# Root steps with a per-partition scalar in place of a second tensor, and a fill that begins on zeros

## The chip, the cores and the metric

One core of a Trainium2 chip runs the whole kernel as one program. The metric is the device time of one execution in microseconds (us), the median of the runs shown. A core has five engines that run beside each other, each through its own instructions in order: TensorE (PE, matrix products; loading of its weights is shown apart as PEld), VectorE (DVE), ScalarE (ACT), GpSimd (POOL) and SyncE (SP, which here issues nearly all transfers). They wait for one another by semaphores.

## The reference

Attention over 2048 tokens of width 1024 (32 heads of 32), gated by a mixture-of-depths feed-forward of eight routed tokens; both work on the layer-normalised input.

```python
xn = _layernorm(x, axis=-1)            # (x - m) / sqrt(v + 1e-5)
s = _A_ref(xn, A_wqkv, A_wo)           # softmax attention, then @ wo
g = _silu(_B_ref(xn, B_w_r, B_w_gate, B_w_up, B_w_down))   # top-8 tokens through a SwiGLU FFN
return x + s * g
```

## The kernel before, in words

The 2048 tokens are 16 tiles of 128 (t = 0 to 15), four tiles to a block. The instructions of all engines are put in order by hand: what Python calls first stands first in its engine's queue.

**The head**, the first 81 us, normalises the tiles and turns them so that features lie on partitions, in two half-precision parts (a high part and a residue, the low part). For each tile `ln_stats` takes mean and variance on DVE (two instructions of 512 columns and one that merges them), `ln_root` makes 1/sqrt(var + eps), `ln_apply` normalises (tile 0 on DVE, the others on ACT). `ln_root` starts with a square root on ACT and returns a list of short DVE steps, run one after the other by `rest()`: a reciprocal y of the root, then vy = (var + eps) * y, w = -0.5 * vy * y, r = (w + 1.5) * y, which is one Newton step, and nmr = -mean * r. From tile 4 on (`wide`) a last step `by` scales r and nmr by 64 with one TENSOR_SCALAR of two columns (L181). All of them work on 128 partitions and one column, `by` on two.

Tiles 0 to 3 are turned by PE (`ln_turn`). Tiles 4 to 15 are turned by DMA: `ln_high` writes the high part on ACT (L217), `ln_turn_dma` lets POOL subtract it from the tile (L223, a two-input TENSOR_TENSOR of 128 x 1024) and then issues a transposing DMA on SP (L226).

One pass of the loop over t in `_fast` calls, in this order: `ln_apply(t+1)`, the square root of tile t+2, `ln_high(t+1)`, PE's products that are due, then `rest()` (the DVE steps of tile t+2), the low part of an early tile, `ln_turn_dma(t+1)`, `ln_stats(t+3)`, the moves (stores and loads on SP that had become due) and the evictions of finished products. So ACT has the square root of one tile in front of the high part of the tile before it; DVE has a tile's steps in front of the next tile's statistics; SP has the transpose in front of stores and loads.

PE meanwhile makes keys, queries and values of the first heads from the turned tiles (`chain`, `chain_v`), in the order of the tiles. Where it has nothing yet, filling products are put: `turn_over(count)` multiplies the identity with itself into a PSUM tile that nobody reads, 13 times before the first tile, then 9 and 6 times more. An fp32 product runs as two passes, so 13 of them are 26 instructions.

**The rest**, from 81 us on, loops over 8 groups of four heads, 4 blocks of queries and 16 tiles of keys: scores on PE, exponentials on ACT, a running sum on DVE, values on PE, with projections, the feed-forward and the output projection put in between.

The identity is built on DVE at the very start, by seven doubling additions, a transposition and a comparison. The pool tag `o32` has two buffers, first used by the attention's output at the end of the first block of queries.

Of the kernel before, what the change touches and what calls it, by code (L numbers as in the profile page):

```python
# [9 lines left out]
F32 = mybir.dt.float32  # L10
# [4 lines left out]
ALU = mybir.AluOpType  # L15
# [3 lines left out]
P = 128  # L19
# [6 lines left out]
EPS = 1e-5  # L26
# [29 lines left out]
@with_exitstack  # L56
def kernel(ctx, tc, x, wqkv, wo, w_r, w_gate, w_up, w_down, out,
                                      general=True, force_general=False):
    nc = tc.nc
    x = x.rearrange("b s d -> (b s) d")  # L60
    out = out.rearrange("b s d -> (b s) d")

    dram = ctx.enter_context(tc.tile_pool(name="dram", bufs=1, space=bass.MemoryType.DRAM))
    keep = ctx.enter_context(tc.tile_pool(name="keep", bufs=1))
    y_d = dram.tile([C, D], F32, name="y_d")
    slot_d = dram.tile([P, NT], I32, name="slot_d")
    ok_i = keep.tile([P, 1], I32, name="ok_i")

    with ExitStack() as st:
        _fast(st, tc, x, wqkv, wo, w_r, w_gate, w_up, w_down, out, dram, y_d, slot_d, ok_i,  # L70
              force_general)

    if general:
        ok = nc.values_load(ok_i[0:1, 0:1], min_val=0, max_val=P)
        with tc.If(ok < P):
            with ExitStack() as st:
                _general(st, tc, x, wqkv, wo, out, dram, y_d, slot_d)
# [28 lines left out]
def _fast(ctx, tc, x, wqkv, wo, w_r, w_gate, w_up, w_down, out, dram, y_d, slot_d, ok_i,  # L106
          force_general):
    nc = tc.nc
    const = ctx.enter_context(tc.tile_pool(name="const", bufs=1))
    sb = ctx.enter_context(tc.tile_pool(name="sb", bufs=1))  # L110
# [4 lines left out]

    ident = const.tile([P, P], F32, name="ident")
    num = sb.tile([P, 2, P], F32, name="num", tag="rb", bufs=1)
    nc.vector.memset(num[:, 0, 0:1], 0.0)  # L120
# [14 lines left out]
    rstd_r, nmr = rn[:, 0], rn[:, 1]  # L135
# [13 lines left out]
    def wide(t):  # L149

        return t >= T_DMA
# [20 lines left out]
    def ln_root(t):  # L172

        tmp = small.tile([P, 4], F32, name="rsq", tag="rsq", bufs=3)
        root, y, vy, w = (tmp[:, i:i + 1] for i in range(4))
        mean, var, r = mv_r[:, t, 0:1], mv_r[:, t, 1:2], rstd_r[:, t:t + 1]
        stt = nc.vector.scalar_tensor_tensor
        nc.scalar.activation(root, var, AF.Sqrt, bias=eps, scale=1.0)
        if wide(t):
            by[t] = small.tile([P, 2], F32, name="by", tag="by", bufs=2)  # L180
        more = [lambda: nc.vector.tensor_scalar(by[t], rn[:, :, t], XS, None, op0=ALU.mult)] if wide(t) else []  # L181
        return [lambda: nc.vector.reciprocal(y, root),
                lambda: stt(vy, var, EPS, y, op0=ALU.add, op1=ALU.mult),
                lambda: stt(w, vy, -0.5, y, op0=ALU.mult, op1=ALU.mult),
                lambda: stt(r, w, 1.5, y, op0=ALU.add, op1=ALU.mult),
                lambda: stt(nmr[:, t:t + 1], mean, -1.0, r, op0=ALU.mult, op1=ALU.mult)] + more

    def ln_apply(t, act):
        xn = LN[t]
# [624 lines left out]
    for g in range(NG):  # L814
        n = g + 1
# [143 lines left out]

    warm = psm.tile([P, 4, P], F32, name="warm", tag="m")  # L960

    def turn_over(count):
        for n in range(count):
            nc.tensor.matmul(warm[:, n % 4, :], ident, ident, start=True, stop=True)

    turn_over(13)

    load_x(0)
    load_x(1)
# [15 lines left out]

    ln_stats(0)
    steps += ln_root(0)
    for _ in range(4):
        step1()
    ln_apply(0, False)  # L990
    step1()
    w_high(1, 0)
    ln_stats(1)
    steps += ln_root(1)
    rest()
    ln_turn(0)
    turn_over(9)
    ln_apply(1, True)
    w_low(1, 0)
# [6 lines left out]
    todo += ks[2:3]  # L1006
    run(400)
    turn_over(6)
    ln_stats(2)
    steps += ln_root(2)  # L1010
    w_low(2, 0)
    rest()
# [281 lines left out]
```

## Time and profile before

| | us |
|---|---|
| median of 3 runs | 1621.5 |
| lowest and highest | 1621.48, 1623.89 |
| the profiled execution | 1622.08 |
| its span, first to last instruction | 1620.2 |
| mean granted clock of TensorE in it | 0.999 of full speed |

The span is shorter than the execution's time by what lies before its first and behind its last instruction. Times in the rows below are counted from the start of the span.

### The profile page before, as it was taken

Reading aid. Unit: us, or ns where it says so; the run is one execution under the profiler, and the core shown is the slowest. Engines: PE = TensorE matmul, PEld = TensorE weight load, DVE = VectorE, ACT = ScalarE, POOL = GpSimd, SP = SyncE. Lnnn points to the kernel's source line nnn. Section 1 sums busy time; section 2 is a strip of 40 time slices with the busy share of each in tenths; the row PEclk is TensorE's granted clock in tenths of the full one; section 3 lists DMA queues with packets and bytes.
Section 4 is the critical chain, followed back from the end, with each engine's and each line's share of the span. In section 5 each row is a group of like instructions: output and inputs, shape, how many; then the busy total and the mean of one; then the engine's idle time right before and its main releaser. Section 6 shows DMA issues by size and latency. Waiting matters only on the chain.

```text
span 1620.2 us, 59634 instructions
## 1 busy us (share of the span) xinstructions
PE 1604.8 (99%) x27193; PEld 816.8 (50%) x27193; DVE 1399.5 (86%) x1128; ACT 1177.2 (73%) x1312; POOL 148.2 (9%) x145
## 2 busy tenths in 40 slices
PE   8999999999999999999999999999999999999998
PEld 7744444444454444444455555555444444455555
DVE  8578999999999998898998988888898999987872
ACT  6677778777787777787877887677777878665530
POOL 3400000000000000000000000000000102030310
PEclk9999999999999999999999999999999999999999
DMA  9935555455644454556655577689788888656533
GB/s 292 203 105 139 140 150 149 135 138 140 176 126 90 116 144 124 138 152 162 170 137 138 137 219 204 173 227 236 209 226 218 236 216 222 212 143 187 180 127 120
DMA packets 250109, 273.68 MB, mean 169 GB/s; under 512 B 107994, under 2 KB 196362, under 8 KB 246010
## 3 DMA queue, kind: packets, MB, share of 16 engines
q1 hardware_dynamic: 239338, 242.10, 51.6%
q0 software_dynamic: 10512, 27.70, 10.8%
q8 instruction: 214, 3.51, 0.9%
q14 instruction: 45, 0.37, 0.1%
HBM read 195.98 MB, written 103.34 MB: 185 GB/s over the span
## 4 chain that ended last, share of the span: by engine, by line
PE 90%; DMA 4%; issue 3%; DVE 2%; SPq 1%; ACT 1%; POOL 0%; POOLq 0%; ACTq 0%; DVEq 0%
PE sc L276 25%; PE oa L421 25%; PE proj L276 17%; PE wop L276 10%; PE vp L276 8%; DMA a_d<-a_d 2%; PE ffn L638 1%; PE vp L323 1%; DMA a_d<-pt 1%; DMA xt<-xh 1%; PE py L669 1%; DMA wraw<-in_A_wqkv_dram 0%; DVE stt L168 0%; DMA wd<-in_B_w_down_dram 0%; PE proj L300 0%
## 5 line engine op out<-in xcount | busy, mean ns | idle before, releaser
L407 ACT ACTIVATE pt<-sc 128x1024 f32<-128x1024 f32 x1024 | 998.3, 1025 | 333.3 <-PE sc L276 249.8
L414 DVE TENSOR_TENSOR pt<-pt 128x2048 f32<-128x2048 f32 x480 | 1095.8, 2285 | 53.2 <-ACT pt L407 30.4
L276 PE MATMUL sc<-qs,ks 128*32 128x512 f16 x8192 | 617.2, 379 | 1.2 <-ACT pt L407 1.2
L421 PE MATMUL oa<-pt,v 128*32 128x512 f32 x4096 | 530.2, 592 | 0.0
L276 PE MATMUL proj<-xt,w 128*32 128x512 f16 x5664 | 417.4, 379 | 0.0
L276 PEld LDWEIGHTS <-ks 128*32 128x32 f16 x8192 | 226.5, 97 | 171.4 <-issue 19.8
L276 PEld LDWEIGHTS <-w 128*32 128x32 f16 x5664 | 155.9, 97 | 238.4 <-issue 139.2
L457 POOL DMA_DIRECT2D a_d<-a_d x90 | 73.0, 811 | 1242.6 <-DMA a_d<-pt 926.0
L276 PEld LDWEIGHTS <-xt 128*32 128x32 f16 x4608 | 125.3, 97 | 108.2 <-issue 79.5
L421 PEld LDWEIGHTS oa<-pt,v 128*32 128x32 f32 x4096 | 127.1, 110 | 100.6 <-ACT o L432 0.4
L276 PE MATMUL wop<-wo,ot 128*32 128x512 f16 (+1 forms) x3168 | 172.7, 373 | 0.0
L276 PE MATMUL vp<-w,xt 128*32 128x256 f16 x4608 | 172.1, 273 | 0.0
L276 PEld LDWEIGHTS <-ot 128*32 128x32 f16 x3168 | 94.2, 97 | 87.2 <-issue 22.4
L374 DVE SCALAR_TENSOR_TENSOR hl<-proj,hl 128x512 f16<-128x512 f32 x61 | 42.0, 689 | 57.6 <-ACT hl L373 57.5
L788 DVE SCALAR_TENSOR_TENSOR z<-wop,z 128x512 f32<-128x512 f32 (+1 forms) x33 | 21.9, 669 | 39.7 <-PE wop L276 39.7
L323 PE MATMUL vp<-w,xt 128*128 128x256 f16 x384 | 43.9, 273 | 2.7 <-DMA xt<-xh 2.6
L323 PEld LDWEIGHTS <-xt 128*128 128x128 f16 x384 | 37.1, 98 | 8.8 <-DMA xt<-xh 3.3
L373 ACT ACTIVATE hl<-proj 128x512 f16<-128x512 f32 x61 | 36.3, 595 | 4.8 <-PE proj L276 3.6
L638 PE MATMUL ffn<-wf,xst 128*32 128x224 f32 x512 | 35.7, 352 | 0.0
L638 PEld LDWEIGHTS ffn<-wf,xst 128*32 128x32 f32 x512 | 16.1, 110 | 38.8 <-issue 37.4
L260 DVE SCALAR_TENSOR_TENSOR w<-wraw,w 128x1024 f16<-128x1024 f32 x23 | 28.0, 1217 | 5.0 <-ACT w L255 5.0
L499 DVE SCALAR_TENSOR_TENSOR ohl<-o,ohl 128x512 f16<-128x512 f32 x28 | 19.3, 690 | 11.9 <-ACT ohl L497 11.9
(145 smaller groups left out, 589.8 us busy)
## 6 DMA issues: line engine op xcount, KB each, us to landing
a_d<-pt SPq DMA_DIRECT2D x30, 1024.0 KB
st<-hl SPq DMA_DIRECT2D x64, 256.0 KB
ks<-st SPq DMA_DIRECT2D x128, 128.0 KB
qs<-st SPq DMA_DIRECT2D x128, 128.0 KB
a_d<-a_d POOLq DMA_DIRECT2D x30, 512.0 KB, 6.6
wf<-in_B_w_gate_dram SPq DMA_DIRECT2D x32, 448.0 KB
wf<-in_B_w_up_dram SPq DMA_DIRECT2D x32, 448.0 KB
wd<-in_B_w_down_dram SPq DMA_DIRECT2D x32, 448.0 KB
```

The lines of the kernel that those rows point to most:

```text
L260: nc.vector.scalar_tensor_tensor(hl[:, 1], WR[c, g], WS, hl[:, 0], op0=ALU.mult, op1=ALU.subtract)
L276: nc.tensor.matmul(out[c], w[:, c], x, **flags)
L323: nc.tensor.matmul(box["ps"][:, tt], xt[:, xi, k, t % 4 * P:(t % 4 + 1) * P], w[:, :, wi, k, :], start=(n == 0), stop=(n == 23))
L373: nc.scalar.activation(hl[:, 0], ps, AF.Copy, scale=KQ)
L374: nc.vector.scalar_tensor_tensor(hl[:, 1], ps, KQ, hl[:, 0], op0=ALU.mult, op1=ALU.subtract)
L407: nc.scalar.activation(PT[u][:, 2 * hf:2 * hf + 2], ps, AF.Exp, bias=0.0, scale=ESC)
L414: nc.vector.tensor_add(ACC[g, qb], ACC[g, qb], PT[u])
L421: nc.tensor.matmul(OA[g, qb][32 * j:32 * j + 32, :], VT[g, kt // 2][:, kt % 2, 32 * j:32 * j + 32], PT[u][:, j, :], start=(kt == 0), stop= ...
L457: nc.gpsimd.dma_start(a_d[0:n], a_d[n:2 * n], accum_op=ALU.add, max_dma_last_dim=4096)
L499: nc.vector.scalar_tensor_tensor(hl[:, 1], o32, OS, hl[:, 0], op0=ALU.mult, op1=ALU.subtract, accum_out=lo_f[:, n:n + 1])
L638: nc.tensor.matmul(box[i][32 * j:32 * j + 32, :], RT["xst"][:, k, :], wt[:, j * FQ:(j + 1) * FQ], start=(k == 0), stop=(k == KT - 1))
L788: nc.vector.scalar_tensor_tensor(z, box[nh][:, c0:c0 + width], WOD, z, op0=ALU.mult, op1=ALU.mult)
```

## The change

Two edits. In `ln_root` the four steps between the reciprocal and `by` become `tensor_scalar` in place of `scalar_tensor_tensor`: the last operand, a column of 128 values, is read as a per-partition scalar and not as a second tensor. And the first filling products no longer multiply the identity but a tile of zeros, `blank`, which DVE writes as its first instruction in a buffer of the tag `o32`; there are 14 of them in place of 13. The two later fills stay on the identity.

```diff
+    blank = sb.tile([P, P], F32, name="blank", tag="o32", bufs=2)
+    nc.vector.memset(blank, 0.0)
     ident = const.tile([P, P], F32, name="ident")
...
-        stt = nc.vector.scalar_tensor_tensor
+        ts = nc.vector.tensor_scalar
...
         return [lambda: nc.vector.reciprocal(y, root),
-                lambda: stt(vy, var, EPS, y, op0=ALU.add, op1=ALU.mult),
-                lambda: stt(w, vy, -0.5, y, op0=ALU.mult, op1=ALU.mult),
-                lambda: stt(r, w, 1.5, y, op0=ALU.add, op1=ALU.mult),
-                lambda: stt(nmr[:, t:t + 1], mean, -1.0, r, op0=ALU.mult, op1=ALU.mult)] + more
+                lambda: ts(vy, var, EPS, y, op0=ALU.add, op1=ALU.mult),
+                lambda: ts(w, vy, -0.5, y, op0=ALU.mult, op1=ALU.mult),
+                lambda: ts(r, w, 1.5, y, op0=ALU.add, op1=ALU.mult),
+                lambda: ts(nmr[:, t:t + 1], mean, -1.0, r, op0=ALU.mult, op1=ALU.mult)] + more
...
-    def turn_over(count):
+    def turn_over(count, src=ident):
         for n in range(count):
-            nc.tensor.matmul(warm[:, n % 4, :], ident, ident, start=True, stop=True)
-
-    turn_over(13)
+            nc.tensor.matmul(warm[:, n % 4, :], src, src, start=True, stop=True)
+
+    turn_over(14, blank)
```

## Rows read from the trace of the kernel before

**Rows 1.** The page's busy times by engine, with shares of the span and numbers of instructions.

```profile
PE 1604.8 (99%) x27193; PEld 816.8 (50%) x27193; DVE 1399.5 (86%) x1128; ACT 1177.2 (73%) x1312; POOL 148.2 (9%) x145
```

**Rows 2.** The waits of PE over the whole span: who waited for whom, us in total, times, the longest.

```profile
PE vp L323 <- DMA xt<-xh: 2.6, 2, 1.4
```

**Rows 3.** The chain of waits over the first 100 us, in order of time: start, us, what. A DMA's time is from its issue to its landing.

```profile
38.68 6.22 DMA xt<-xh
...
75.76 5.36 DMA xt<-xh
...
81.17 2.79 PE vp L323 x24
```

**Rows 4.** The timeline of one turn of the head, of all engines but PE: start, us, engine, line, operation, out<-in, count, and in brackets the idle time before it and what ended it. The steps belong to tile 6, POOL's subtraction to tile 5.

```profile
32.12 0.29 ACT L178 ACTIVATE rsq<-mv_r,eps 128x1 f32<-128x1 f32 x1 [1.16 <-DVE mv_r L170]
32.33 1.04 ACT L217 ACTIVATE xh<-xin 128x1024 f16<-128x1024 f32 x1
32.45 0.16 DVE L182 RECIPROCAL rsq<-rsq 128x1 f32<-128x1 f32 x1 [0.36 <-ACT rsq L178]
...
33.42 0.17 DVE L181 TENSOR_SCALAR by<-rn 128x2 f32<-128x2 f32 x1
33.44 2.15 POOL L223 TENSOR_TENSOR xh<-xin,xh 128x1024 f16<-128x1024 f32 x1 [1.92 <-DVE rn L186]
...
35.06 0.29 ACT L178 ACTIVATE rsq<-mv_r,eps 128x1 f32<-128x1 f32 x1 [0.19 <-DVE mv_r L170]
```

**Rows 5.** Line L181 by itself: how often, duration in ns (least, median, most), first and last start in us.

```profile
L181 DVE TENSOR_SCALAR by<-rn x12: 169/169/2056, 25.2 to 63.8; 128x2 f32<-128x2 f32 x12
```

**Rows 6.** The timeline of the last two turns, columns as in rows 4.

```profile
58.69 2.12 POOL L223 TENSOR_TENSOR xh<-xin,xh 128x1024 f16<-128x1024 f32 x1 [0.80 <-ACT xh L217]
58.78 2.06 DVE L181 TENSOR_SCALAR by<-rn 128x2 f32<-128x2 f32 x1
...
62.50 0.29 ACT L178 ACTIVATE rsq<-mv_r,eps 128x1 f32<-128x1 f32 x1
...
63.80 0.17 DVE L181 TENSOR_SCALAR by<-rn 128x2 f32<-128x2 f32 x1
63.81 2.15 POOL L223 TENSOR_TENSOR xh<-xin,xh 128x1024 f16<-128x1024 f32 x1 [3.00 <-DVE rn L186]
...
66.47 2.13 POOL L223 TENSOR_TENSOR xh<-xin,xh 128x1024 f16<-128x1024 f32 x1 [0.51 <-ACT xh L217]
```

**Rows 7.** DVE's groups by line and shape over the whole span: count, then busy us, mean ns of one, and idle us before them. L516 is the routing's dot product, whose scalar is the tile's mean; L744 has an immediate. L677 multiplies by a per-partition gate; L644 and L1131 have immediates. L184 is a root step.

```profile
L744 DVE SCALAR_TENSOR_TENSOR z<-up,z 128x1024 f32<-128x1024 f32 x16 | 19.4, 1220 | 3.7 <-ACT up L743 3.7
...
L516 DVE SCALAR_TENSOR_TENSOR xr<-xr,mv_r,wr_bc 128x1024 f32<-128x1024 f32 x16 | 20.4, 1278 | 0.0
...
L184 DVE SCALAR_TENSOR_TENSOR rsq<-rsq 128x1 f32<-128x1 f32 x16 | 2.5, 159 | 0.6
...
L644 DVE TENSOR_SCALAR fe<-fe 128x224 f32<-128x224 f32 x4 | 1.1, 273 | 0.3 <-ACT fe L643 0.3
...
L677 DVE TENSOR_SCALAR y<-y,gate 128x256 f32<-128x256 f32 x1 | 0.4, 353 | 0.0
...
L1131 DVE TENSOR_SCALAR fl<-fl 128x1 f32<-128x1 f32 x1 | 0.1, 147 | 0.0
```

**Rows 8.** The timeline around POOL's two instructions on a weight tile (L265 with one tensor input, L266 with two), columns as in rows 4.

```profile
19.56 2.82 POOL L265 TENSOR_SCALAR wraw<-wraw 128x1024 f32<-128x1024 f32 x1 [19.10 <-ACT w L255]
...
21.57 0.16 DVE L183 SCALAR_TENSOR_TENSOR rsq<-mv_r,rsq 128x1 f32<-128x1 f32 x1
...
22.46 2.14 POOL L266 TENSOR_TENSOR w<-wraw,w 128x1024 f16<-128x1024 f32 x1
...
24.37 0.25 DVE L183 SCALAR_TENSOR_TENSOR rsq<-mv_r,rsq 128x1 f32<-128x1 f32 x1
```

**Rows 9.** The timeline of the first turn with a subtraction on POOL, columns as in rows 4; the square root is tile 5's.

```profile
28.06 0.29 ACT L178 ACTIVATE rsq<-mv_r,eps 128x1 f32<-128x1 f32 x1 [1.13 <-DVE mv_r L170]
...
29.36 0.17 DVE L181 TENSOR_SCALAR by<-rn 128x2 f32<-128x2 f32 x1
29.38 2.14 POOL L223 TENSOR_TENSOR xh<-xin,xh 128x1024 f16<-128x1024 f32 x1 [4.77 <-ACT xh L217]
```

**Rows 10.** SP's queue between the transposes of tiles 14 and 15: start and us of the issuing, columns as in rows 4.

```profile
72.91 2.15 SPq L389 DMA_DIRECT2D ks<-st  x4
75.11 0.54 SPq L332 DMA_DIRECT2D v_d<-vs  x1
```

**Rows 11.** A stretch behind tile 4's transpose: its length, then busy us (and instructions) of each engine, the granted clock, the busy share of the DMA engines, GB/s.

```profile
35.50:36.00 0.50, 0.50 (x4) 0.24 (x3) 0.40 (x4) 0.50 (x1) 0.09 (x1) 1.00 0.00 0
```

**Rows 12.** The timeline of the start, columns as in rows 4.

```profile
0.82 0.06 DVE L120 MEMSET num<- 128x1 f32 x1 [0.82 <-PEq L1283]
0.86 0.09 DVE L130 MEMSET ones<- 128x32 f32 x1
...
3.19 4.57 PE L964 MATMUL warm<-ident 128*128 128x128 f32 x26 [3.19 <-DVE ident L126]
...
3.78 0.69 DVE L168 BATCH_NORM_STATS2 stt<-xin 128x6 f32<-128x512 f32 x1 [0.64 <-DMA xin<-in_A_x_dram]
```

**Rows 13.** The filling passes by themselves, between 5 and 5.5 us and between 6.5 and 7 us: count, duration in ns (least, median, most), first and last start.

```profile
L964 PE MATMUL warm<-ident x5: 421/421/421, 4.6 to 5.5; 128*128 128x128 f32 x5
...
L964 PE MATMUL warm<-ident x7: 275/275/275, 6.3 to 6.9; 128*128 128x128 f32 x7
```

## The prediction

> **What bounds the kernel now.** I read the page's busy shares first. TensorE (PE) is busy for 1604.8 of 1620.2 us [rows 1], and in the waits of PE the only long ones are for the identity at the start [rows 12] and for two landings of transposed tiles [rows 2]. So what the change does to the time is what it does to the moment at which PE gets its last input of the head (the first 81 us); after that PE's order is fixed and nearly gapless, and a shift at 81 us goes through to the end. I then read the chain of waits over the head. Up to 33 us it runs through VectorE (DVE): the root steps of tile after tile, with the statistics between them; then through GpSimd's subtraction (POOL, L223), SP's queue and the transposes. PE waits last at 81.17 us, for the landing of tile 15, whose transpose SP issued at 75.76 us, 5.41 us earlier [rows 3].
>
> Next I read the timeline of one tile's turn, where the changed steps stand [rows 4]. At 32.12 ACT starts a square root; call that moment s. At s+0.20 ACT starts the high half of the tile before (L217), which ends at s+1.24, and POOL's subtraction starts 0.08 later, at s+1.32. Meanwhile DVE does the reciprocal (s+0.33), four short steps and "by" (L181) at s+1.30. So "by" starts 0.02 us ahead of POOL. It is so in ten turns of eleven, from 29.36 against 29.38 in the first to 63.80 against 63.81 in the last, never by more than 0.04 [rows 6, 9]. In the eleventh a DVE eviction had come between, and "by" started at 58.78, 0.09 us after POOL at 58.69. It took 2.06 us, until 60.84, when POOL's 2.12 were over [rows 6]; the median of L181 is 169 ns [rows 5]. On that view I stake the forecast: "by" that comes in front of POOL is free, "by" that comes behind it waits for the whole subtraction.
>
> **The change part by part: the steps.** Four steps of each of 16 roots become TENSOR_SCALAR with one immediate and one per-partition scalar. The trace has no such form with one column, so I bound it. TENSOR_SCALAR with immediates alone takes 147 ns at one column; the old form takes 159. What a per-partition scalar adds is seen at other sizes. SCALAR_TENSOR_TENSOR of 1024 columns takes 1278 ns with one and 1220 without: +58. TENSOR_SCALAR of 256 columns with one takes 353, and 224 columns without take 273: +80, or +42 if the 32 columns more cost 1.2 ns each, the other operation's rate (1220 over 1024) [rows 7]. So a step takes 147 ns at the least and 147+80 = 227 at the most. I take 209, as the closest pair (one operation, one size, with and without) says about 60: +50 ns a step, 0.20 us a root.
>
> **What 0.20 us a root costs by itself.** Tile 0's root is hidden behind a weight split on ACT. Roots 1 to 4 lie on the chain: 0.80 us, less 0.09 because tile 4's first step at 24.37 lasted 0.25 (it ended with POOL's L266) [rows 8] and would now start as that ends. So s of tile 5 moves from 28.06 [rows 9] to about 28.8.
>
> **What it costs through POOL.** From there on "by" would start at s+1.50 and POOL still at s+1.32, since POOL waits for ACT's L217, which waits for nothing of DVE's behind s. So "by" ends with POOL, at s+1.32+2.14+0.02 = s+3.49 instead of s+1.47: 2.02 us later, in each of the ten turns that escaped until now. Behind "by" on DVE stand the next tile's statistics, behind these the next square root; ACT waits for "by" with the tile's normalisation. From the end of "by" to the next square root it is 1.47 us [rows 4], so the period becomes 4.95, against 2.94 where DVE alone set it. Other turns were longer, as ACT's evictions stood in them; these now fit into ACT's new wait, so I count periods and not additions. From tile 5 to tile 6 it was 4.06 (a residue step stands behind "by") and becomes 6.08 [rows 4, 9]. Then come nine periods of 4.95, and tile 15's square root starts at 28.8+6.1+44.6 = 79.5, against 62.50. Its "by" is held too, and from the end of "by" (63.97) to the end of POOL's last subtraction (68.60) it is 4.63 [rows 6]: 79.5+3.49+4.63 = 87.6, +19.0.
>
> The row at 58.78 shows a two-column TENSOR_SCALAR held; it doesn't show whether one column is held too, which would add 0.25 us a turn if the last step came late. [...]
>
> Of the 19 us SP has covered some: it issued tile 15's transpose at 75.76, 7.16 us after POOL, since its queue ran late. With tiles 5 us apart it no longer does. Behind tile 14's transpose (POOL ends at 82.9, and some 2.2 us of issue) come four loads of keys (2.15), a store (0.54) and small gaps, to 88.0 [rows 10]. So the issue is at about 88, +12.2. To landing it was 5.36 us in a busy queue and 6.22 in the longest case [rows 3]; tile 4's, alone in the queue, was issued from POOL's end at 31.52 [rows 9], and by 35.5 its traffic was over [rows 11]: 4.0 us. PE starts tile 15 at 92.0 to 94.3, +10.8 to +13.1; it has by then done the rest, tile 14's products included. I take +12.
>
> **The fill.** A blank tile is set first on DVE; 32 columns take 0.09 us and one takes 0.06, so a column costs about 1 ns and 128 take 0.16 to 0.2. The identity is that much later, and the DVE idles 0.64 us for the first input behind it: hidden. PE starts at about 1.05 instead of 3.19 [rows 12]. [...] The old fill's 26 passes took 4.57 us, up to 7.76, where the first transposes follow; 28 passes that begin 2.1 us sooner end before that at any rate. Nothing is gained, as PE is not awaited there. The loss could be a clock that falls in the idleness of some 2 us that now lies before the transposes: the next 18 passes at half speed add 1.9 us at most, and the evictions behind them have slack. I put it at nothing and keep 1 us for the range.
>
> **Sum.** +12 on the profiled 1622.08 (span 1620.2 and 1.9 around it) is 1634.1; that execution lies 0.6 over the median 1621.5, so 1633.5.
>
> **Rivals.** (1) The steps get dearer, but POOL doesn't hold "by": one row shows the holding, and "by" there came 0.09 behind, not 0.18. Then six roots on the chain up to tile 6 cost 0.20 each, and SP and PE carry 1.2 us to the end: 1622.7, no change. Against it: the row's 2.06 us end within 0.03 of POOL's. (2) The other side: steps as cheap as with immediates, 147 instead of 159. "by" stays in front, six roots give back 0.3 us, and the 0.09 at 24.37 as well: 1621.1. The point that decides is small: 0.01 to 0.04 us over four steps, so a step dearer by more than 3 to 10 ns puts "by" behind POOL. For it speaks that the old steps read two tensors and the new ones one, and that the one old step that met POOL's two-input L266 was held, while the steps from 21.57 on ran freely beside the one-input L265 [rows 8]. Against it, +58 and +42 to +80. [...] (3) Only some turns collide. The trace names DVE as POOL's releaser in three turns, as at 33.44 and 63.81 [rows 4, 6]; I read these as ACT's end, which lies 0.08 before each start, but if POOL waits for L186 there, three of ten escape, 2 us each: about 1627.5. (4) More than I sum: the last step before "by" is held as well (+0.25 a turn, +2.5), or PE's clock falls in its new waits of 2 us a tile (+1 to 3): up to 1637.5.
>
> **How the numbers follow.** The forecast, with (4) as its upper end, 1630 to 1637.5, has 0.78; (3) 0.06; (1) 0.09; (2) 0.05; something that makes it faster 0.02. The forecast's own range leaves out a little over 2 in 10, so the range reaches down to (1): 1622.3 to 1637.5. With 0.2% (3.2 us, about what a measurement here can tell from none): slower 0.84, same 0.14, faster 0.02.
>
> **What would show it.** The steps at L183 to L186 at 0.20 to 0.21 us; "by" at L181 with a median near 2 us, 11 of 12 long; DVE's busy time up by some 22 us and POOL's unchanged; square roots 4.95 us apart; SP's last transpose near 88 us; PE's waits for landings at some 12 us more; the first product near 1.05 us. I am wrong if the steps last 160 ns or less, if "by" stays at 0.17, or if PE's main part regains what the head lost.

## The result and the profile after

The changed kernel took 1635.32 us (median of 6 runs, 1634.21 to 1640.34) against 1621.49 for the kernel before on the same chip (6 runs, 1620.42 to 1623.89). The ratio is 1.0087, with a 95% interval of 1.0072 to 1.0101: slower by 13.8 us, where 12 had been forecast (1633.5 us, range 1622.3 to 1637.5). The profiled execution of the changed kernel took 1634.23 us, its span is 1632.5: 12.3 more than before. New lines of code shift the numbers by two: "by" is L183 now, the four steps L185 to L188, the square root L180, POOL's subtraction L225, SP's transpose L228, the values' products L325.

The page's busy times, to be held against [rows 1]:

```profile
PE 1610.6 (99%) x27195; PEld 808.5 (50%) x27195; DVE 1419.7 (87%) x1129; ACT 1177.6 (72%) x1312; POOL 145.7 (9%) x145
```

DVE has 20.2 us more, POOL 2.5 less (only 0.2 of that in the head). Where DVE's time went is seen in its groups by line and shape over the first 110 us (busy us, mean ns of one, idle us before):

```profile
L183 DVE TENSOR_SCALAR by<-rn 128x2 f32<-128x2 f32 x12 | 21.2, 1770 | 0.4
...
L187 DVE TENSOR_SCALAR rn<-rsq 128x1 f32<-128x1 f32 x16 | 3.4, 214 | 0.6
L186 DVE TENSOR_SCALAR rsq<-rsq 128x1 f32<-128x1 f32 x16 | 3.4, 214 | 0.6
```

A step takes 214 ns, 55 more than the old form's 159 [rows 7]. And "by", which took 169 ns eleven times out of twelve before, now takes 1770 in the mean. Its line by itself (least, median, most) beside [rows 5], with who waited for it:

```profile
L183 DVE TENSOR_SCALAR by<-rn x12: 168/1942/1950, 26.3 to 81.0; 128x2 f32<-128x2 f32 x12
...
  ACT xin L194: 20.7, 11
```

The timeline of one turn, the counterpart of [rows 4] (start, us, engine, line, operation):

```profile
35.14 0.30 ACT L180 ACTIVATE rsq<-mv_r,eps 128x1 f32<-128x1 f32 x1 [1.32 <-DVE mv_r L172]
...
36.41 0.21 DVE L188 TENSOR_SCALAR rn<-mv_r,rn 128x1 f32<-128x1 f32 x1
36.45 2.12 POOL L225 TENSOR_TENSOR xh<-xin,xh 128x1024 f16<-128x1024 f32 x1 [3.94 <-DVE rn L187]
36.66 1.94 DVE L183 TENSOR_SCALAR by<-rn 128x2 f32<-128x2 f32 x1
38.64 1.24 ACT L194 ACTIVATE xin<-xin,by 128x1024 f32<-128x1024 f32 x1 [2.26 <-DVE by L183]
...
40.07 0.29 ACT L180 ACTIVATE rsq<-mv_r,eps 128x1 f32<-128x1 f32 x1 [0.19 <-DVE mv_r L172]
```

POOL starts 1.31 us behind the square root, as before. "by" starts 1.52 behind it, 0.21 us after POOL, and ends at 38.60, 0.03 after POOL's 38.57. ACT gets the next tile's scalars two microseconds late, and the next square root comes 4.93 us after this one instead of 2.94 [rows 4]. From here the chain of waits carries it to PE; its part from 76 us on, beside [rows 3]:

```profile
76.20 1.84 DVE by L183
78.04 1.20 DVE stt L170 x2
79.27 0.22 DVE mv_r L172
79.51 0.30 ACT rsq L180
...
80.83 2.13 POOL xh L225
82.98 1.34 SPq L228
84.41 1.25 SPq L391
...
87.81 5.62 DMA xt<-xh
93.48 2.79 PE vp L325 x24
```

PE starts the last tile's products at 93.48 in place of 81.17, 12.31 us later. From there to the end of the span it is 1539.0 us in both kernels (1632.5 less 93.48; 1620.2 less 81.17). So the whole loss lies in the head, and nothing behind it is faster or slower.

### The profile page after: what moved, and what is told of

It is laid out like the page before. It is cut to its first block, busy times and chain, and to the rows that moved or that the text cites. A ratio compares the mean times of both kernels' runs of the same rounds, so it can differ in the third digit from the quotient of the medians.

```text
span 1632.5 us, 59639 instructions
## 1 busy us (share of the span) xinstructions
PE 1610.6 (99%) x27195; PEld 808.5 (50%) x27195; DVE 1419.7 (87%) x1129; ACT 1177.6 (72%) x1312; POOL 145.7 (9%) x145
## 4 chain that ended last, share of the span: by engine, by line
PE 92%; DVE 4%; DMA 2%; ACT 1%; issue 0%; SPq 0%; POOL 0%; ACTq 0%; POOLq 0%
PE sc L278 27%; PE oa L423 26%; PE proj L278 18%; PE wop L278 10%; PE vp L278 8%; PE ffn L640 1%; DVE by L183 1%; DVE stt L170 1%; PE py L671 1%; DMA wf<-in_B_w_gate_dram 0%; DMA wraw<-in_A_wqkv_dram 0%; ACT pt L409 0%; DMA a_d<-pt 0%; DMA xt<-xh 0%; PE proj L302 0%
## 5 line engine op out<-in xcount | busy, mean ns | idle before, releaser
L278 PEld LDWEIGHTS <-ks 128*32 128x32 f16 x8192 | 222.4, 97 | 174.8 <-issue 19.0
L278 PEld LDWEIGHTS <-w 128*32 128x32 f16 x5664 | 152.4, 97 | 242.0 <-issue 140.4
L325 PE MATMUL vp<-w,xt 128*128 128x256 f16 x384 | 46.2, 279 | 10.3 <-DMA xt<-xh 8.1
L325 PEld LDWEIGHTS <-xt 128*128 128x128 f16 x384 | 37.5, 100 | 18.2 <-DMA xt<-xh 9.9
```

The source lines that it names most:

```text
L278: nc.tensor.matmul(out[c], w[:, c], x, **flags)
L325: nc.tensor.matmul(box["ps"][:, tt], xt[:, xi, k, t % 4 * P:(t % 4 + 1) * P], w[:, :, wi, k, :], start=(n == 0), stop=(n == 23))
```

## The experiments

The theory: the two-column "by" is free in front of POOL's subtraction and held behind it; four steps of +50 ns put it behind; each held "by" costs one longer turn. Its rivals: the fill does it; or it is the steps' own time alone (six roots on the chain, 1.2 us); or the steps are held themselves. On the chips of these runs the kernel before took 1621.9 us.

**The two edits apart.** The first kernel is the kernel before with the four steps exchanged, the second the changed kernel with the four steps put back.

```diff
-        stt = nc.vector.scalar_tensor_tensor
+        ts = nc.vector.tensor_scalar
...
-                lambda: stt(vy, var, EPS, y, op0=ALU.add, op1=ALU.mult),
+                lambda: ts(vy, var, EPS, y, op0=ALU.add, op1=ALU.mult),
...
```

> The four root steps as TENSOR_SCALAR with a per-partition scalar, the first fill as before (13 products on the identity). The theory (a held step: L181, the two-column by, falls behind POOL's subtraction and waits for it) puts the whole difference here: by at a median of about 1.94 us, 10 or 11 of 12 long, square roots 4.93 us apart, span about 12 us over before, 1633 to 1635 us. A rival that blames the fill (PE idle between the zeros and the first transposes, or its clock) expects 1622 to 1623 here.

> The fill alone: 14 products on a tile of zeros, the steps as before. The theory expects 1621.5, within 0.5 of before: PE begins 2 us sooner and is not awaited there; by stays in front of POOL at 169 ns. The rival that blames the fill expects some 1633 here.

The steps alone took 1634.87 us, ratio 1.0079 (1.0062 to 1.0096); the fill alone 1621.92, ratio 1.0004 (0.9995 to 1.0014). In the first "by" takes 1769 ns in the mean (1770 in the changed kernel), in the second 326, one held of twelve, as before. So the fill is worth nothing that these runs can tell, and the steps explain the loss.

**"by" on one column at a time.** The changed kernel, its last step as two instructions of one column each, on the same data, at the same place:

```diff
-        more = [lambda: nc.vector.tensor_scalar(by[t], rn[:, :, t], XS, None, op0=ALU.mult)] if wide(t) else []
+        more = [lambda i=i: nc.vector.tensor_scalar(by[t][:, i:i + 1], rn[:, i, t:t + 1], XS, None, op0=ALU.mult)
+                for i in range(2)] if wide(t) else []
```

> The changed kernel, but by made as two one-column steps in place of one two-column step. If only the two-column form is held by POOL (the last root step, with one column, began behind POOL in three turns of the changed kernel and took 0.214 us as ever), by falls behind POOL and is yet not held: nothing at 1.9 us, turns of about 3.2 to 3.3 us where they were 4.93, and what is left is the dearer steps, 1622.5 to 1623.5. A rival that blames the dearer per-partition steps themselves, or anything in POOL that holds each later step, expects 1633 to 1636.

It took 1623.61 us, ratio 1.0014 (1.0004 to 1.0024), 0.1 above the range that was expected; the turns that DVE sets took 3.15 us (square roots at 52.72 and 55.87). "by" starts behind POOL's subtraction and isn't held. First DVE's group, then a turn's timeline (DVE and POOL):

```profile
L183 DVE TENSOR_SCALAR by<-rn 128x1 f32<-128x1 f32 x24 | 3.2, 149 | 0.0
```

```profile
29.88 2.13 POOL L226 TENSOR_TENSOR xh<-xin,xh 128x1024 f16<-128x1024 f32 x1 [5.10 <-ACT xh L220]
...
29.96 0.27 DVE L183 TENSOR_SCALAR by<-rn 128x1 f32<-128x1 f32 x2
```

All of the dear steps are still in this kernel, and one instruction more. What is gone is the shape of "by", and with it 12.1 of the 13.8 us (each against the kernel before on its own chip). That is the holding, shown by itself. What is left over, 1.7 us, is about what the prediction's first rival had for a change without holding (1.2); in the trace PE starts the last tile at 82.90, 1.73 us later than before.

**A delay of another make, one and two of them.** The kernel before with neutral one-column steps (w times 1.0) between the old ones, in the tiles from 4 on. They delay "by" without any per-partition scalar.

```diff
+        slow = [lambda: nc.vector.tensor_scalar(w, w, 1.0, None, op0=ALU.mult)] * (1 if wide(t) else 0)
...
+                *slow,
```

> The kernel before, with one step more in the roots of tiles 4 to 15: w is multiplied by 1.0 (a one-column TENSOR_SCALAR with immediates, about 0.18 us with its gap), so by starts about 0.16 us behind POOL. No per-partition scalar is read that was not read before. The theory expects by held at about 1.95 us, turns of 4.93 us, and nearly all of the loss: 1632.5 to 1634, some 0.7 under the changed kernel, as roots 1 to 3 are not dearer. The rival that blames the scalar reads expects the 0.18 us of three roots at most: 1622.

> The kernel before with two such neutral steps in the roots of tiles 4 to 15. Now L186's step, a SCALAR_TENSOR_TENSOR that reads two tensors of one column, starts about 0.15 us behind POOL as well. If POOL's two-input subtraction also holds what reads two tensors from SBUF, this step lasts about 2 us and by behind it 0.17; if it holds the two-column step alone, L186 stays at 0.16 and by lasts about 1.8. In either case the time is 1633 to 1635.

With one step it took 1634.27 us, ratio 1.0081 (1.0064 to 1.0098): 12.4 us more than before, close to the loss of the change and 0.3 above the expected range, from a delay of 0.19 us by other means. So the form of the steps isn't the cause; the order against POOL is. But in three of the turns another instruction had the wait, the old last step, which reads two tensors of one column (timeline of DVE and POOL):

```profile
44.75 2.12 POOL L225 TENSOR_TENSOR xh<-xin,xh 128x1024 f16<-128x1024 f32 x1 [2.81 <-ACT xh L219]
...
44.83 2.06 DVE L188 SCALAR_TENSOR_TENSOR rn<-mv_r,rn 128x1 f32<-128x1 f32 x1
46.92 0.17 DVE L181 TENSOR_SCALAR by<-rn 128x2 f32<-128x2 f32 x1
```

With two neutral steps it came to 1639.08 us where 1633 to 1635 was expected, a miss; it is a single run, so it has no interval. Of the two cases that the expectation named, the first came: "by" was never held (169 ns in each of its twelve), and the two-tensor step in front of it was, in eight turns the last one and in three even the one before it:

```profile
46.08 2.13 POOL L225 TENSOR_TENSOR xh<-xin,xh 128x1024 f16<-128x1024 f32 x1 [3.00 <-ACT xh L219]
...
46.15 2.07 DVE L187 SCALAR_TENSOR_TENSOR rn<-rsq 128x1 f32<-128x1 f32 x1
48.26 0.16 DVE L188 SCALAR_TENSOR_TENSOR rn<-mv_r,rn 128x1 f32<-128x1 f32 x1
48.45 0.17 DVE L181 TENSOR_SCALAR by<-rn 128x2 f32<-128x2 f32 x1
```

The expectation had both cases end at the same time, and there it failed: what stands behind the held instruction is added to the turn. The nine turns from tile 6 to tile 15 took 5.12 to 5.33 us each (34.51 to 81.23) where the changed kernel's took 4.93 (35.14 to 79.51). So POOL's last subtraction ended later, and the transpose of tile 15 was issued at 89.57 instead of 87.81. That is 1.8 us; the products of tile 15 took 4.46 us instead of 2.79, another 1.7 (more on this below). Of the 4.8 us between the two spans (1637.3 and 1632.5) 1.3 are left, and PE's waits behind the head show them: it waited 1.6 us for weights of the feed-forward (rows below), 0.3 in the changed kernel. No root step stands there.

```profile
PE ffn L640 <- DMA wf<-in_B_w_up_dram: 1.0, 1, 1.0
...
PE py L671 <- DMA wd<-in_B_w_down_dram: 0.6, 2, 0.4
```

**Only the late tiles.** The kernel before with the new form of the steps for tiles 10 to 15 alone.

```diff
-        stt = nc.vector.scalar_tensor_tensor
+        stt = nc.vector.tensor_scalar if t >= 10 else nc.vector.scalar_tensor_tensor
```

> The steps as TENSOR_SCALAR with a per-partition scalar for tiles 10 to 15 only, fill as before. Five turns are newly held, about 2 us each on DVE. The theory says that SP's queue covers the first part of it: POOL's last subtraction ends near 77.8 us instead of 68.6, but SP's last transpose goes out at 78.0 to 78.5 instead of 75.8: 1623.5 to 1624.5. A rival that gives each held turn its share of the 12.3 us lost by ten expects 1627 to 1628.

It took 1626.28 us, ratio 1.0025 (1.0015 to 1.0035): above the theory's 1623.5 to 1624.5, under the 1627 to 1628 of an even share by turns. The timeline of POOL gives the last subtraction, and the chain of waits settles where the time differs:

```profile
76.05 2.13 POOL L223 TENSOR_TENSOR xh<-xin,xh 128x1024 f16<-128x1024 f32 x1 [2.52 <-ACT xh L217]
```

```profile
78.41 6.29 DMA xt<-xh
...
84.75 4.46 PE vp L323 x24
```

POOL's end (78.18) and the issue on SP (78.41) came where the theory had put them (77.8; 78.0 to 78.5): six held turns move POOL by 9.6 us and the issue by 2.65, since SP's late queue covers the rest. But the transfer took 6.29 us in place of 5.36, and then the 24 products took 4.46 in place of 2.79 [rows 3]: 2.65 + 0.93 + 1.67 = 5.25, of 5.4 in the spans (1625.6 less 1620.2). The profiled execution was the slowest of eight; the medians are 4.4 us apart. Two rows on these products, from PE's timeline (in brackets PE's idle time before them) and from their window (length; busy us of PE, PEld, DVE, ACT, POOL; granted clock; DMA share; GB/s), first here, then in the changed kernel, then in the kernel with one neutral step:

```profile
84.75 4.46 PE L323 MATMUL vp<-w,xt 128*128 128x256 f16 x24 [2.77 <-DMA xt<-xh]
...
84.75:89.21 4.46, 4.46 (x28) 3.18 (x32) 0.00 (x0) 0.51 (x1) 0.00 (x0) 0.62 0.56 165
```

```profile
93.48 2.79 PE L325 MATMUL vp<-w,xt 128*128 128x256 f16 x24 [2.05 <-DMA xt<-xh]
...
93.48:96.27 2.79, 2.79 (x28) 2.33 (x32) 0.00 (x0) 0.65 (x1) 0.00 (x0) 1.00 0.32 113
```

```profile
92.31 2.79 PE L325 MATMUL vp<-w,xt 128*128 128x256 f16 x24 [2.19 <-DMA xt<-xh]
...
92.31:95.10 2.79, 2.79 (x28) 2.32 (x32) 0.00 (x0) 1.99 (x3) 0.00 (x0) 1.00 0.39 129
```

The granted clock is 0.62 in the first of them, after PE had stood idle for 2.77 us waiting for the landing. That is nearer the 0.50 that the changed kernel shows from 69 to 72 us, behind a wait of 2.82 us in the head, than 1.00. In front of the last tile PE stood idle for 2.05 in the changed kernel and the clock stayed at 1.00. The steps-only run (2.48 idle) and the run with two neutral steps (2.15) show 0.62 as well, and the run with the split "by" (2.18) 0.64, with 4.18 us for the products. But with one neutral step PE stood idle for 2.19, longer than in two of these, and the clock stayed at 1.00. So the length of the wait alone doesn't decide it. The lower clock costs 1.7 us, and I had left it out of the expectation for this kernel, which therefore came out too low. No run was made to find what decides it.

**Without "by".** A version meant to be safe: from tile 4 on the square root works on (var + eps) / 4096, so that the steps give 64r and 64 times nmr at once, "by" is gone, and one division behind the head gives back the unscaled ones.

```diff
+            nc.scalar.activation(root, var, AF.Sqrt, bias=eps2, scale=1.0 / XS ** 2)
...
+                    lambda: stt(b0, w, 1.5, y, op0=ALU.add, op1=ALU.mult),
+                    lambda: stt(b1, mean, -1.0, b0, op0=ALU.mult, op1=ALU.mult)]
...
+    nc.vector.tensor_scalar(rn[:, :, T_DMA:], rn[:, :, T_DMA:], 1.0 / XS, None, op0=ALU.mult)
```

> A version meant to be safe from the collision: tiles 4 to 15 take the square root of (var + eps)/4096, so that the steps make 64 r and 64 nmr directly; by is gone and one step after the head divides all of them by 64. The first step is a one-column TENSOR_SCALAR with a per-partition scalar, as it stands where POOL may still be at work. Theory: no step of 1.9 us, turns of 2.8 us where DVE sets them, and 0.3 to 0.6 us less at the last transpose: 1621.0, hard to tell from before. If a two-tensor step is caught behind POOL here, some turns lengthen by up to 2 us and it ends at 1622 to 1630.

It took 1621.86 us, ratio 0.9999 (0.9990 to 1.0008), the same as before. No step is held, the last transpose is issued at 75.30 (75.76 before) and PE starts the last tile at 80.78 (81.17). It gains nothing that can be measured: the kernel before lost only one turn of eleven to POOL, and PE's last start is only 0.39 us sooner without that. No version that beats the kernel before was found.

## Why the prediction was right, and where it was off

**The steps.** Forecast 209 ns, bounds 147 and 227; measured 214. A per-partition scalar thus adds 67 ns at one column to the 147 of immediates alone [rows 7], where the pair of 1278 and 1220 ns at 1024 columns had given 58; the estimate was 5 ns short. Rival (2), steps as cheap as with immediates, fails on this row.

**The holding.** Forecast: "by" long in 11 of 12, median near 2 us. Measured: median 1942 ns, 11 times, ended by POOL's end within 0.03 us. The one row at 58.78 of the kernel before [rows 6] was the rule and not an accident, and rival (1) falls.

**The turns.** Forecast square roots 4.95 us apart; 4.93 measured. Tile 5's at 28.8, tile 15's at 79.5, POOL's end at 87.6, SP's issue near 88, PE between 92.0 and 94.3; measured 29.08, 79.51, 87.61, 87.81 and 93.48. That 79.5 was met to the hundredth is in part luck: tile 5's square root came 0.3 us late (0.25 of it from ahead of the first root on the chain, at 10.57 instead of 10.32), and ten turns that were each 0.02 shorter than forecast made up for most of it. Rival (3), three turns that escape because POOL waits for DVE, fails: the trace names DVE L187 as POOL's releaser in the turn at 36.45 above too, and "by" is held in it all the same.

The prediction's reading of the chain of waits leaves out a piece: in the middle of the head it runs through PE's products and ACT's evictions, and not through transposes alone.

```profile
44.95 5.41 PE vp L323 x48
50.37 5.18 PE projw L300 x24
55.55 5.25 PE vp L323 x48
...
60.82 0.38 ACT v L329
```

So before the change many of DVE's turns had slack (3.38 us each from 32.12 to 62.50, against 2.94 where DVE alone set the pace). In the changed kernel the chain stays on the turns up to 80.76, and tile 15's square root moved by 17.0 us, less than tile 5's 1.0 and the nine new holds ahead of it (2.0 us each) added up. Counting whole periods, as the prediction did, takes this in.

**A one-column step that comes late** (rival 4). In three turns the last step started behind POOL; one of them, timeline of DVE and POOL:

```profile
46.32 2.12 POOL L225 TENSOR_TENSOR xh<-xin,xh 128x1024 f16<-128x1024 f32 x1 [2.81 <-ACT xh L219]
...
46.38 0.21 DVE L188 TENSOR_SCALAR rn<-mv_r,rn 128x1 f32<-128x1 f32 x1
46.62 1.84 DVE L183 TENSOR_SCALAR by<-rn 128x2 f32<-128x2 f32 x1
```

The one-column step runs through in 0.21 us, in the middle of POOL's subtraction; the two-column one behind it is held. So the 2.5 us that the prediction kept for its upper end didn't come. The 149 ns of the split "by" agree with this. Why the two-column step is held and the one-column one isn't, no run shows.

**The relief** that rival (2) counted as 0.09 us at one place, for reading one tensor instead of two, was sized much too low. It is a whole hold: the old step, late, is held 2.06 us (one neutral step), the new one, late, isn't. It did not help here, because the two-column "by" stands behind it and is held instead. With two tensors a step is held on one column too: 2.06 us with one neutral step, 2.07 with two. Beside POOL's one-input instruction on a weight tile such steps ran at 0.16 us (from 21.57 on [rows 8]).

**Signs that were wrong.** PE's waits for landings were to be 12 us longer; they rose by 5.5 only. The rows of the changed kernel's waits of PE, beside [rows 2]:

```profile
PE vp L325 <- DMA xt<-xh: 8.1, 5, 2.8
PE vp L325 <- DVE xt L233: 2.2, 2, 2.0
```

Two rows show the head up to the last tile's products, before and after (window; length; busy us of PE, PEld, DVE, ACT, POOL; granted clock; DMA share; GB/s):

```profile
0.00:81.17 81.17, 73.89 (x632) 58.79 (x633) 53.27 (x174) 50.33 (x72) 30.84 (x18) 1.00 1.02 248
...
0.00:93.48 93.48, 79.63 (x635) 62.21 (x635) 73.83 (x175) 52.01 (x73) 30.62 (x18) 0.96 0.87 215
```

PE is idle for 13.85 us in place of 7.28, 6.6 of the 12.3; the other 5.7 are its own work that became longer under cover of the late tiles. 1.7 of that is the first fill, the rest mostly products for values and projections, with a granted clock of 0.83, 0.93 and 0.90 in the windows 30:40, 60:70 and 70:80, against 1.00 before. PE at the lower clock fills time in which it would have waited. The clock of rival (4) thus fell, but in the head, where the last landing decides and not PE's work. Only behind the last landing does it cost, 1.7 us, and it did so in some of the profiled runs (above) but not in that of the changed kernel.

**The fill.** PE starts it at 1.07 us (1.05 forecast). The idle time of some 2 us before the transposes didn't come; in the timeline of the start

```profile
1.07 6.29 PE L966 MATMUL warm<-blank 128*128 128x128 f32 x28 [1.07 <-DVE eps L136]
...
8.01 1.09 PE L205 MATMUL xtp<-ident,xin 128*128 128x128 f32 x8 [0.65 <-DVE xin L196]
```

it is 0.65: the 28 passes took 6.29 us, a pass 425 ns in the mean and none under 368, so none ran at the 275 that [rows 13] show towards the end, though the granted clock reads 1.00 here as before (0 to 8 us). Behind the 0.65 us it reads 1.00 as well (8 to 20 us); the half speed that the prediction feared is seen later in the head, the 0.50 from 69 to 72 us. The zeros needn't be the reason for the long passes: in the steps-only run 26 passes on the identity took 5.70 us (4.57 before), in the fill-only run the 28 took 5.85. How long the passes of [rows 13] take is thus one execution's value, and what sets it was not shown. The fill's worth of nothing stands.

**Why 13.8 and not 12.** The profiled pair differs by 12.15 us (1634.23 against 1622.08). The medians differ by more, since the profiled execution of the kernel before lay 0.6 above its median and that of the changed kernel 1.1 below its own. That some executions also have the slower products behind the last landing would explain the latter, but is only argued: the other executions have no trace.

## What to carry over

Before making a step of a short dependent chain dearer, look at what it races: here 0.2 us per tile cost 2 us per tile, because the last instruction lost a race against another engine that it had won by 0.02 us. One long duration of an otherwise short instruction in a trace (most 2056, median 169) is a warning of such a race; what else started just before it tells against whom. The cure that was shown is the instruction's shape: the same work on one column at a time was not held (149 ns an instruction), though it still came late. The number of tensor inputs counts in the same way: a late one-column step with two tensors was held (2.06 us), one with a single tensor was not (0.21 us).

## What the runs showed of the hardware

- Beside POOL's two-input subtraction of 128x1024 (2.12 us) a two-column fp32 TENSOR_SCALAR that started later was held until 0.03 us after its end, and so was a SCALAR_TENSOR_TENSOR with two tensors of a single column (2.06 us); a one-column TENSOR_SCALAR was not, with immediates (149 ns) or with a per-partition scalar (214 ns). Which came first decides: 0.02 us ahead was free. Beside POOL's one-input instruction (2.82 us) steps with two tensors ran at 0.16 us [rows 8].
- A per-partition scalar in place of an immediate cost 67 ns at one column (214 against 147) and 58 at 1024 [rows 7]. Against the two-tensor form (159) the new step is 55 ns dearer.
- A wait of PE in front of the last tile costs more than itself in some runs: behind 2.15, 2.48 and 2.77 us of idleness the granted clock was 0.62 and the 24 products took 4.46 us, behind 2.05 and 2.19 it was 1.00 and they took 2.79. The wait of 2.19 kept the clock and that of 2.15 lost it, so its length alone doesn't decide; what does was not found.
